# Two places of TensorE's program order in a long-convolution and soft-MoE kernel: transposes of the logits ahead of the inverse transform's first product, and the logits' products directly behind the dispatch products

## The chip, the core and the metric

The kernel runs on one NeuronCore of a Trainium2 chip. The core has TensorE (PE, matrix products; PEld is its weight load), VectorE (DVE), ScalarE (ACT), GpSimd (POOL), and SyncE (SP), whose queue issues nearly all DMA transfers here. The metric is the device time of one execution in microseconds (us). Three runs of the kernel before gave 859.84, 865.26 and 866.72 us; their median is 865.26 us.

## The reference

A batch of 8 sequences of 5696 tokens with 128 channels is convolved with a filter of the same length through Fourier transforms; the 45568 rows that result go through a soft mixture of experts with 32 slots. Everything is float32.

```python
Xf = np.fft.rfft(x, n=2 * S, axis=1); Hf = np.fft.rfft(h, n=2 * S, axis=0)
x = np.fft.irfft(Xf * Hf[None], n=2 * S, axis=1)[:, :S, :].reshape(B * S, D)
logits = x @ phi                          # (45568, 32)
d = np.exp(logits - logits.max(0)); d /= d.sum(0) + 1e-9
slot_input = d.T @ x                      # dispatch: sums over all tokens
for e in range(8): slot_out[e] = np.maximum(slot_input[e] @ w1[e], 0) @ w2[e]
c = np.exp(logits - logits.max(1)); c /= c.sum(1) + 1e-9
return c @ slot_out
```

## The kernel before

The transform of length N is split into 90 times 64 points and worked in three stages, each a set of matrix products on TensorE with a round through DRAM between them. The work is a software pipeline over steps t. The program order on every engine is the order in which the Python code issues instructions (a manual schedule), and each engine works its own list from the front.

**First stage** (`load_x`, `fold`, `first_low`, `first_high`; lines 195 to 226). Four columns of the input are loaded (L195), folded into sums and differences on GpSimd (L207), multiplied with a table (L217), copied out of PSUM by ScalarE into `fst` (L220) and stored to DRAM as `f` (L226).

**Second stage** (`stage_b1`, `stage_b2`). A unit loads `gt` from `f` (L249), makes products into the PSUM tile `bt` (L263), is multiplied with the filter's spectrum by four VectorE operations (two at L281, two at L290, ending in `yf`), is multiplied back on TensorE (L305), copied by ScalarE into `zst` (L311) and stored as `z` (L314). `slot_b` issues the first half of a new unit and then the second half of the unit before it, so the second half has to wait for `yf`. There are three units in two steps: one slot in an odd step, two in an even one. Each batch ends on a short unit of a quarter of the products.

**Third stage and soft MoE**, for a pair T of column groups, in two steps. In the odd step `stage_c1` waits for `zc` (L342, five DMAs of 1.15 MB in all into one single buffer), makes four products of two matrix products each (L361) in two parts, copies one half of each part with ScalarE (L370 into `y`, L374 into `om`) and combines the halves on VectorE (lines 366 and 367, once for `y`, once for `op` and `om`); GpSimd makes the rest of `y` (L380). In the even step `stage_c2` transposes `y` (L391, copies L393 into `yt`), `stage_c6` transposes the weights of the pair before the last (L504, copies L508), `dispatch` makes the slot sums of the pair before (L478, added by VectorE at L483), `stage_c3` makes the logits from `yt` and `phi` (L400, ScalarE copy into `lt` at L403), and `column_max` takes the running maximum over tokens on VectorE (L411, L416 into `low`, L419 into `df`). In the next odd step `stage_c4` transposes `lt` (L429), copies it into `L` (L433), takes the exponential `dt` with `low` as bias (L435) and that of `df` (L440), has GpSimd clear a corner of `dt` (L437), takes the maximum over slots on VectorE (L444) and subtracts it on GpSimd (L445). `stage_c5` transposes `dt` (L452, copy L455), and `softmax` finishes `L` (L460 to L466).

The order inside a step is given by strings of letters, one letter for one piece of the work, `ORDER_E` for odd steps and `ORDER_O` for even ones from step 9 on: `x` load of the input, `X` and `Y` first-stage products, `f` folds, `1`, `j` and `w` the first products, the second products and the combination of `stage_c1`, `4`, `b` (`slot_b`), `5`, `s` (softmax), `z` load of `zc`, `P` load of `gt`, `2`, `6`, `d` (dispatch), `3`, `m` (column maximum). Letters whose work does not exist in a step issue nothing. First-stage work ends before step 72; steps 72 to 79 still run second and third stage, and the step after them and the rest of the kernel (experts, output) are written out by hand.

All these products but L263's go to four rotating PSUM banks (`bank()`), so a bank is free once the reader of the tile four allocations earlier has finished.

Of the kernel before, what the change touches and what calls it, by code (L numbers as in the profile page):

```python
# [77 lines left out]
def kernel(  # L78
# [484 lines left out]
    for comp in range(2):  # L563
        fold(0, comp)
    wait_b2 = []
    ORDER_E, ORDER_O, FILL_E, FILL_O, XAHEAD = "xXYf14jwb5s", "zPxXfb26db3m", "xYfX14jwb5s", "zPxfXb26db3m", 3

    for t in range(last_front + 1):
        us = list(units(t))
# [286 lines left out]
```

## Time and profile before

| what | value |
|---|---|
| median of three runs | 865.26 us |
| the profiled execution's own time, and its span | 866.74 us, 864.4 us |
| busy in the span: PE, DVE, ACT, POOL | 89%, 72%, 51%, 43% |
| mean granted TensorE clock | 0.947 |
| moved by DMA | 271.99 MB, mean 315 GB/s |
| chain that ended last, by engine | PE 58%, DMA 21%, DVE 12%, SP's queue 3% |

A row of the timeline gives the start of a group of like instructions, its duration, engine, line, operation, tiles and count, and in brackets the idle time of the engine ahead of it with what ended that idle time. Matrix products overlap, so the time that a group takes on TensorE is read from its start to the start of the next group. A float32 product appears as two instructions, which is why eight are listed for four products.

### The profile page before, as it was taken

How to read it: one execution, taken by the hardware profiler on the slowest of the kernel's cores; microseconds unless marked ns; L12 is line 12 of the kernel's file. 1: busy time of each engine (PE TensorE's matmuls, PEld its weight loads, DVE VectorE, ACT ScalarE, POOL GpSimd, SP SyncE). 2: the span in 40 equal slices, each digit the busy share in tenths (PEclk: the TensorE clock that was granted, in tenths of full speed). 3: DMA queues.
4: the chain of work that ended last, by engine and by line, in shares of the span. 5: the costliest groups of instructions: out<-in, count | busy, mean ns of one | idle time of the engine just before them, and what ended most of it. 6: DMA issues, size and time to landing. Idle time of an engine off the chain costs nothing.

```text
span 864.4 us, 20502 instructions
## 1 busy us (share of the span) xinstructions
PE 769.7 (89%) x7796; PEld 374.4 (43%) x7796; DVE 626.5 (72%) x942; ACT 437.4 (51%) x967; POOL 374.8 (43%) x359
## 2 busy tenths in 40 slices
PE   5878888779999999999999999999978878978882
PEld 1222333234444444444444444444444444445882
DVE  3259867658777878887888788877778997973542
ACT  3422344435655655665566556656544545562531
POOL 2133424245556556665566555555533443540000
PEclk9999999989999999999999999999999999997755
DMA  9989999999999999999999999999997797760998
GB/s 294 294 268 308 306 319 342 337 335 331 329 323 343 343 349 318 343 337 340 325 336 345 320 339 330 348 312 335 334 333 264 265 316 277 283 276 8 371 380 327
DMA packets 153243, 271.99 MB, mean 315 GB/s; under 512 B 11878, under 2 KB 110054, under 8 KB 150005
## 3 DMA queue, kind: packets, MB, share of 16 engines
q1 hardware_dynamic: 152571, 270.38, 90.5%
q8 instruction: 62, 1.02, 0.4%
q10 hardware_dynamic: 576, 0.31, 0.1%
q14 instruction: 34, 0.28, 0.1%
HBM read 142.57 MB, written 127.98 MB: 313 GB/s over the span
## 4 chain that ended last, share of the span: by engine, by line
PE 58%; DMA 21%; DVE 12%; SPq 3%; issue 2%; ACT 1%; POOL 1%; DVEq 0%; ACTq 0%; POOLq 0%
PE bank L217 14%; PE bank L361 13%; PE bank L305 8%; PE bt L263 7%; PE bank L391 5%; DMA zc<-z 5%; DMA xc<-in_x_dram 5%; DMA out_dram<-o 5%; PE bank L478 3%; DMA gt<-f 3%; DMA xc<-in_h_dram 2%; DVE yf L290 2%; SPq L342 2%; DVE p L281 2%; DVE bt L281 2%
## 5 line engine op out<-in xcount | busy, mean ns | idle before, releaser
L207 POOL TENSOR_TENSOR x<-xc 128x512 f32<-128x512 f32 x126 | 158.0, 1276 | 245.0 <-PE bank L217 177.0
L217 PE MATMUL bank<-x,s 128*64 128x512 f32 (+1 forms) x1152 | 224.6, 610 | 14.0 <-DVE x L207 9.2
L311 ACT ACTIVATE zst<-bank 128x512 f32<-128x512 f32 (+1 forms) x184 | 98.6, 586 | 184.3 <-PE bank L305 165.1
L220 ACT ACTIVATE fst<-bank 128x512 f32<-128x512 f32 x216 | 127.4, 598 | 106.3 <-PE bank L217 87.6
L281 DVE TENSOR_TENSOR p<-bt,Hi 128x1024 f32<-128x1024 f32 x96 | 111.3, 1160 | 32.7 <-PE bt L263 31.6
L361 PE MATMUL bank<-zc,i 128*64 128x512 f32 x480 | 119.1, 618 | 12.4 <-DMA zc<-z 10.0
L305 PE MATMUL bank<-yf,vt 64*64 64x256 f32 x1440 | 100.8, 387 | 25.7 <-DVE yf L290 25.6
L263 PE MATMUL bt<-gt,wt 64*64 64x256 f32 x1620 | 114.3, 389 | 9.6 <-DMA gt<-f 8.1
L290 DVE TENSOR_TENSOR yf<-bt,p 128x512 f32<-128x512 f32 x192 | 119.4, 663 | 3.3
L217 PEld LDWEIGHTS bank<-x,s 128*64 128x64 f32 (+1 forms) x1152 | 55.8, 124 | 150.3 <-issue 79.9
L281 DVE TENSOR_TENSOR bt<-bt,Hr 128x1024 f32<-128x1024 f32 x96 | 113.0, 1177 | 0.0
L263 PEld LDWEIGHTS bt<-gt,wt 64*64 64x64 f32 x1620 | 54.2, 132 | 84.6 <-issue 33.1
L380 POOL TENSOR_TENSOR y<-y,op 128x512 f32<-128x512 f32 x64 | 77.6, 1212 | 13.4 <-DVE op L366 10.4
L305 PEld LDWEIGHTS bank<-yf,vt 64*64 64x64 f32 x1440 | 56.3, 134 | 57.4 <-issue 23.1
L366 DVE TENSOR_TENSOR y<-bank,y 128x512 f32<-128x512 f32 x32 | 22.1, 692 | 77.3 <-PE bank L361 73.8
L380 POOL TENSOR_TENSOR y<-y,om 128x512 f32<-128x512 f32 x54 | 64.1, 1187 | 2.1
L361 PEld LDWEIGHTS bank<-zc,i 128*64 128x64 f32 x480 | 30.9, 139 | 76.8 <-issue 46.6
L391 PE MATMUL bank<-ident,y 109*128 109x109 f32 x512 | 62.4, 272 | 1.3 <-DVE y L380 1.0
L391 PEld LDWEIGHTS bank<-ident,y 109*128 109x128 f32 x512 | 52.1, 147 | 17.2 <-issue 9.2
L393 ACT ACTIVATE yt<-bank 128x360 f32<-128x360 f32 x128 | 51.0, 490 | 2.4 <-PE bank L391 1.8
L809 PE MATMUL op<-so,cT 32*128 32x128 f32 x704 | 45.9, 379 | 5.7 <-ACT o L818 5.2
L466 POOL TENSOR_TENSOR L<-L,rs 128x512 f32<-128x512 f32 x32 | 33.6, 1051 | 31.1 <-DVE rs L465 20.9
(96 smaller groups left out, 792.0 us busy)
## 6 DMA issues: line engine op xcount, KB each, us to landing
gt<-f SPq DMA_DIRECT2D x99, 512.0 KB
z<-zst SPq DMA_DIRECT2D x88, 512.0 KB
f<-fst SPq DMA_DIRECT2D x144, 240.0 KB
zc<-z SPq DMA_DIRECT2D x30, 1024.0 KB
xc<-in_x_dram SPq DMA_DIRECT2D x64, 320.0 KB
f<-fst SPq DMA_DIRECT2D x144, 120.0 KB
out_dram<-o SPq DMA_DIRECT2D x16, 1024.0 KB
zc<-z SPq DMA_DIRECT2D x90, 128.0 KB
```

Of the source, the lines that this page charges most:

```text
L207: eng.tensor_tensor(out=folded(c, comp)[:, :, :], in0=t_[:, 0, :, :], in1=t_[:, 1, ::-1, :], op=AL.subtract if comp else AL.add)
L217: nc.tensor.matmul(p[o * width:(o + 1) * width, :], s1[:, comp + G, k], folded(c, comp)[:, :, :].rearrange("p n d -> p (n d)"), start=True ...
L220: nc.scalar.activation(st[:, :, G, :], p[:, :].rearrange("p (n d) -> p n d", d=D), AF.Copy)
L263: nc.tensor.matmul(bt[q * HP:(q + 1) * HP, a, o, :], wt[r, 2 * i + q, :], t_[r, 2 * o + q, :, :].rearrange("p c d -> p (c d)"), start=True ...
L281: nc.vector.tensor_tensor(out=p_, in0=pv, in1=h_, op=AL.mult)
L290: eng.tensor_tensor(out=y_[r, 0:k, c, :], in0=pv[:, :, c, :], in1=pi[r, 0:k, 1 - c, :], op=op_)
L305: nc.tensor.matmul(bz[q][a * HP:(a + 1) * HP, o * 2 * D:(o + 1) * 2 * D], vt[r, i, a, :], y_[r, a * m + o, :, :].rearrange("p c d -> p (c ...
L311: nc.scalar.activation(st[:, 0:m, q, :], bz[q][:, 0:m * 2 * D].rearrange("p (o x) -> p o x", o=m), AF.Copy)
L361: nc.tensor.matmul(p[h_ * HP:(h_ + 1) * HP, :], i1[0:kr, tab, :], t_[0:kr, h_, o, :, q, :], start=True, stop=True)
L380: eng.tensor_tensor(out=part_, in0=part(v, 0), in1=o_[:, :, :], op=sign)
L391: nc.tensor.transpose(p[:, i * TR:(i + 1) * TR], ys[T][0:TR, k * CH + i, 0:D], ident[0:TR, 0:TR])
L393: nc.scalar.activation(yt[:, k * CH:(k + 1) * CH, :, :], of_tokens(p), AF.Copy)
```

## The change

Two letters move, each by one place, in the strings for steps from 9 on; the strings for the steps before that are not touched.

```diff
-    ORDER_E, ORDER_O, FILL_E, FILL_O, XAHEAD = "xXYf14jwb5s", "zPxXfb26db3m", "xYfX14jwb5s", "zPxfXb26db3m", 3
+    ORDER_E, ORDER_O, FILL_E, FILL_O, XAHEAD = "xXYf41jwb5s", "zPxXfb26d3bm", "xYfX14jwb5s", "zPxfXb26db3m", 3
```

In odd steps `stage_c4` (L429 to L445) is issued ahead of the first part of `stage_c1` (L361, L370, L366, L367) and no longer between its two parts. On TensorE the eight L361 products become adjacent behind the four L429 transposes. On ScalarE the order L370, L433, L435, L440, L374 becomes L433, L435, L440, L370, L374. On VectorE L444 moves ahead of the first L366 and L367. In even steps `stage_c3` (L400, L403) is issued directly behind `dispatch` (L478) and ahead of the second `slot_b` (L263, L305, L281, L290, L311) and no longer behind it; on ScalarE L403 comes ahead of the two L311, and `column_max` stays behind the slot on VectorE. The lists of GpSimd and of SyncE with its DMAs are the same in both kernels. No instruction is added or removed.

## The prediction

> **What bounds the kernel now.** I read the page's slices first, then busy time by stretch, then the waits of TensorE and of SyncE's queue inside the stretch where all stages run, then the timelines there and in the steps after 72. The slices say that TensorE and the DMA engines are both nearly full from slice 9 to 28, about 190 to 630 us.
>
> ```profile
> PE   5878888779999999999999999999978878978882
> PEclk9999999989999999999999999999999999997755
> DMA  9989999999999999999999999999997797760998
> ```
>
> The busy time by stretch (columns: stretch, its length, then busy time and count of PE, PEld, DVE, ACT, POOL, then clock, DMA share, GB/s), one row for a batch of four pairs and two for a pair each in the steps from 72 on:
>
> ```profile
> 319.36:400.88 81.52, 80.31 (x825) 37.27 (x825) 64.93 (x100) 48.73 (x112) 47.75 (x45) 1.00 0.97 335
> 400.88:482.18 81.30, 80.30 (x824) 37.24 (x825) 65.01 (x100) 48.57 (x111) 47.33 (x45) 1.00 0.97 336
> ...
> 664.30:683.16 18.86, 16.20 (x184) 9.46 (x181) 16.88 (x26) 9.34 (x23) 6.87 (x7) 0.91 0.84 292
> 683.16:701.91 18.75, 16.09 (x185) 8.92 (x181) 16.87 (x26) 9.16 (x23) 6.85 (x7) 0.91 0.88 303
> ```
>
> In the full part a batch takes 81.3 to 81.5 us and TensorE idles about 1.0 us of it; the DMA share is 0.97. Who is ahead of whom is told by the waits of SyncE's queue from 238 to 606 us:
>
> ```profile
> SPq L195 <- DMA gt<-f: 34.5, 27, 2.0
> SPq L314 <- DMA gt<-f: 19.1, 17, 2.1
> SPq L195 <- DMA zc<-z: 16.8, 22, 2.5
> SPq L226 <- DMA z<-zst: 16.0, 23, 1.0
> ```
>
> These and the other rows that name a DMA add up to 117 of 368 us: the queue waits for earlier transfers to land. Rows that name an engine add up to 42 us, but most name one that cannot hold that transfer (a `z` store behind the `y` copy). Those that can (L226 behind its own `fst`, L314 behind `zst`, L195 behind the fold, L249 behind `bt`) are 1.8, 1.5, 2.8 and 0.9 us, 7.0 in all, 4% of the 159. The queue also runs behind the engines: the second slot's `zst` copies of one step were done at 438.1 us and their stores were issued from 441.9 on. So in the full part transfers run at their own pace and TensorE meets them at `zc`: it stood waiting ahead of L361 at 197.85, 218.21, 319.36, 400.88, 482.18, 523.12, 563.83 and 605.71 us for 0.28, 0.41, 0.68, 0.86, 0.66, 0.35, 0.58 and 1.24 us, 5.1 in all.
>
> From 72 on first-stage work is gone and VectorE sets the pace: TensorE idles 2.67 us in each pair until `yf`.
>
> ```profile
> 671.10 1.09 PE L263 MATMUL bt<-gt,wt 64*64 64x256 f32 x16
> 674.86 1.09 PE L305 MATMUL bank<-yf,vt 64*64 64x256 f32 x16 [2.67 <-DVE yf L290]
> ...
> 681.69 1.23 DVE L281 TENSOR_TENSOR p<-bt,Hi 128x1024 f32<-128x1024 f32 x1 [0.66 <-PE bt L263]
> ...
> 686.63 0.61 ACT L435 ACTIVATE dt<-lt,low 128x360 f32<-128x360 f32 x1 [0.31 <-DVE low L416]
> ```
>
> **The change, part by part.** Nothing is added or removed, so a gain can only be a change of geometry saved on TensorE or a wait covered, and a loss something queued behind a wait.
>
> *Products that become neighbours.* TensorE groups are priced from start to start. Four L361 products took 1.87 us ahead of the transposes (421.13 to 423.00) and 1.86 behind them (423.59 to 425.45), 3.73 in all. Late in the kernel, where eight follow one another, they took 3.58:
>
> ```profile
> 739.32 3.65 PE L361 MATMUL bank<-zc,i 128*64 128x512 f32 x16
> 742.90 1.72 PE L391 MATMUL bank<-ident,y 109*128 109x109 f32 x16
> ```
>
> That saves 0.15 us a pair. Dispatch takes 1.03 us ahead of L263 (434.01 to 435.04) and 0.91 in the one place where L400 follows it (718.45 to 719.36); L400 took 0.74 (436.93 to 437.67) and there 0.72. That saves 0.14. The first applies in 22 odd steps (29 to 71), the second in 21 even ones (30 to 70): 22 x 0.15 + 21 x 0.14 = 6.2 us of TensorE's time in the full part. The Trainium skill, "TensorE: Matmul & The Clock Gate", section "The mechanism" of Part 3, says that a weight load overlaps matrix products in flight only when it goes to another row group; by that both pairings, which use all 128 rows, would save nothing, and TensorE's 6.2 us would be 0. The rows above disagree with it.
>
> *Transposes L429 ahead of L361.* They need only `lt`, copied three microseconds earlier, and take 0.59 us (423.00 to 423.59). They move into the wait for `zc`; of the eight waits they can fill 0.28 + 0.41 + 0.59 + 0.59 + 0.59 + 0.35 + 0.58 + 0.59 = 4.0 us.
>
> Together the full part could give 10.2 us at one end. At the other it gives nothing: if the transfers keep their pace, `zc` lands when it did, and what TensorE saves becomes a longer wait ahead of L361. SyncE's list is unchanged and 96% of its waits are for its own transfers, so I am near that end: 4% of 10.2 is 0.4, and I take 0.5 us gained.
>
> *Step 73.* Here `zc` is late by 2.61 us (L361 at 644.75), and the clock is cold behind the wait: the transposes took 1.04 us (647.44 to 648.48). They go into the wait; with the saved change of geometry 1.2 us are gained, between nothing (if a later wait absorbs them) and 1.2. The next late thing is `yf` (656.06, waited for 2.28 us), which hangs on L361's end, so I take 1.2.
>
> *The pairs behind it, steps 74 to 79.* VectorE is busy without a gap from L281 of the second slot (662.83) through the maximum, the combinations and the next unit to `yf` at 674.7, and TensorE's slot waits for that. L400 now stands ahead of the L263 that starts this run: dispatch and L400 take 0.91 + 0.72 instead of dispatch's 1.03, so everything behind is 0.60 us later. Then L370: behind it in the old order stood the exponential L435, which waits for `low`; now L370 stands behind L435. In the row of 664 to 683, counted from L281's start at 662.83, `low` lets L435 start at +4.93, and L440 and then L374 followed at +5.44 and +5.53. L370 now takes that place, ends at +6.13, and VectorE's first L366 starts at +6.16 instead of +4.95. L444 runs inside that delay; the first L366 and L367 take 1.34 us (667.78 to 669.12), so the second L366 starts at +6.16 + 1.34 = +7.50 instead of +6.88 (669.71), 0.62 us later. So 1.22 us a pair, for three pairs (74/75, 76/77, 78/79): 3.7 us lost. The ends: 0 if L370's delay and L400 were covered, which no row suggests, and 2.6 a pair if the wait of 2.67 us, grown to 3.9, doubles the slow-clock stretch behind it (from 675.88 on L391 took 2.47 us where 431.82 to 433.55 shows 1.73, L504 0.87 for 0.46, L478 1.31 for 1.03: 1.4 us more); I take none of that, since the clock already drops at 2.67 us. The skill's same page, section "What's actually happening", puts the drop at an idle window of 3.4 us; by that the longer wait would be what crosses it, and the 1.4 us would come new in each pair, 4.2 us on the sum. The clock of 0.91 in these rows says it is paid already.
>
> *In the full part the same two delays must be checked.* L400 ahead of the slot makes `low` 0.60 us later: 441.0 becomes 441.6, while L435 can start, behind Y's last copy and L433, no earlier than 1.2 us after 441.3. That leaves 0.8 us. L370 then ends some 2.4 us after the transposes begin, when its partner product is just done, and the second L366 waits for its own product as before. The `zst` copies come 0.5 us later and their stores have 3.8 us to spare. PSUM banks: the second L361 product of the second part takes the bank of the transposes, freed by L433 two microseconds before; none is later than its product. I cost all this at nothing; if the 0.8 us were gone, it would be the drain's 0.62 us in every pair.
>
> **Sum**, against the profiled execution's 866.74 us: -0.5 - 1.2 + 3.7 = +2.0, or 868.7 us. That execution lies 1.5 us above the median of the runs shown; against the median the forecast is 867.2, rounded 867 us.
>
> **Rivals.** *The transfers follow TensorE.* If the 3% in which DMA engines rest can be used, a batch may fall from 81.4 towards 79.8 us, and over 5.3 batches up to 8.5 of the 10.2 us come through. For: the share reached 1.00 in single pairs, and a share below it means room. Against: the rows of SyncE's queue, full of waits for landings. With two thirds of it, 6 us: -6 - 1.2 + 3.7 = -3.5 from the median, 861.8, say 862 us. With all 8.5: 859 us. *Slower: L370 behind L435 in every pair.* One mechanism: the column maximum, late on VectorE, holds L435, and L370 and the first L366 queue behind it, so that `yf` is late at the first slot of the even step, where now there is nothing in hand (it stood waiting 0.35 us in one pair of four). It decides once `low` is over 0.8 us later than worked out, or L366's start over 0.4 us more. Price 0.62 x 22 = 13.6 us on top of the forecast: 881 us. For it: the drain shows L435 waiting for `low` by 0.3 us already. Against: VectorE stands idle 2.2 us ahead of the first L366 in the full part (423.19). *It does nothing anywhere*: the drain's delays are covered after all: 865.
>
> **How the numbers follow.** The forecast 0.51, the transfers' case 0.36, the slower case 0.08, nothing 0.05. The likeliest time is 867 us. The range goes from 860 (the transfers' case at most of its size) to 872 (the forecast with the slow-clock stretch, and the beginning of the slower case). A measurement of this kernel tells about 1% from no change. Over 1% faster (below 856.6) needs more than the whole of the transfers' case: 0.04. Over 1% slower (above 873.9) needs the slower case: 0.07. The rest, 0.89, is within 1%.
>
> **What would show it.** Right: batches still of 81.3 to 81.5 us with TensorE's wait ahead of L361 present in nearly every pair, its sum near 5 + 6 us; pairs from 664 us on of about 20.0 us with `yf` waits near 3.9; eight L361 products in 3.58 us; dispatch to L400 in 0.91. Wrong: batches of 80 us with few such waits (the transfers follow), `yf` waits in every even step of the full part (L370), or drain pairs still of 18.8 us.

## Result and profile after

The changed kernel took 867.84 us (median of 17 runs, 861.81 to 870.83), the kernel before, run beside it, 864.64 us (17 runs, 859.70 to 869.74). The ratio of the two is 1.0019 with a 95% interval of 0.9998 to 1.0040: between 0.2 us faster and 3.5 us slower, so no difference that this measurement can tell. The forecast was 867, a loss of 2 us. The profiled execution of the changed kernel took 869.63 us by its own time, with a span of 867.1 us.

Executions of one and the same kernel differ by up to 0.7% to either side. Ratios here and below are taken over all executions in the usual state and are not the quotients of the medians. The totals of single profiles are therefore not ranked below; what is compared is stretches inside them, and the ratios of many runs.

The slices of the page after the change:

```profile
PE   5888788789999999999999999999988778988882
PEclk9999999999999999999999999999999999989755
DMA  9889999999999999999999999999997887760999
```

As before, TensorE and the DMA engines are both nearly full between slices 9 and 28. One number of the page did move: VectorE is busy for 655.2 us instead of 626.5, with the same 942 instructions. That is the first sign of something that the prediction didn't have.

Busy time by stretch (columns as in the prediction: stretch, its length, then busy time and count of PE, PEld, DVE, ACT, POOL, clock, DMA share, GB/s), four batches of the full part and two pairs of the steps after 73:

```profile
237.82:320.12 82.30, 79.49 (x825) 38.03 (x825) 71.54 (x101) 50.40 (x115) 49.30 (x46) 1.00 0.97 332
320.12:400.78 80.66, 79.42 (x824) 38.02 (x825) 70.19 (x99) 48.05 (x109) 45.87 (x44) 1.00 0.97 335
400.78:482.58 81.80, 79.51 (x824) 38.41 (x825) 71.32 (x101) 50.31 (x115) 48.69 (x46) 1.00 0.97 337
482.58:566.60 84.02, 81.02 (x825) 38.70 (x825) 70.50 (x100) 48.07 (x109) 46.25 (x44) 0.98 0.96 326
...
664.27:684.34 20.07, 16.64 (x181) 9.43 (x180) 16.63 (x26) 9.14 (x23) 6.89 (x7) 0.91 0.89 316
684.34:704.41 20.07, 16.64 (x182) 9.64 (x181) 16.63 (x26) 9.25 (x23) 6.88 (x7) 0.91 0.83 283
```

In three of the four batches TensorE works 0.8 us less than the 80.3 of before (by the prediction's prices it would be 4 x 0.29 = 1.2), and the batch is still 81 to 84 us long at the same DMA share. VectorE works 70 to 71.5 us in a batch instead of 65. The pairs after 664 us take 20.07 us instead of 18.8.

For a table I cut both traces at the first L361 of step 29 (the second such group), of step 73 and of step 81. "Full part" is the first interval, "drain" the second, "tail" the rest.

| us | full part | drain | tail | idle ahead of L361 (full part, and step 73) | idle ahead of L305 (full part) |
|---|---|---|---|---|---|
| before | 446.90 | 76.43 | 143.24 | 7.66 in 9 places | 3.54 in 6 |
| after | 447.44 | 79.08 | 142.96 | 8.46 in 9 | 6.48 in 18 |

The start of the full part, 197.85 and 197.65 us, makes up the difference of the spans: -0.20 + 0.54 + 2.65 - 0.28 = +2.7 us. The loss is in the drain, and the full part took none of TensorE's saving. The waits of SyncE's queue from 238 to 606 us still begin with transfers that wait for transfers:

```profile
SPq L195 <- DMA gt<-f: 38.8, 29, 2.2
SPq L195 <- DMA zc<-z: 23.7, 30, 2.1
```

In the drain, the timelines of TensorE, VectorE and ScalarE show both delays that the prediction named:

```profile
675.58 1.73 PE L305 MATMUL bank<-yf,vt 64*64 64x256 f32 x16 [3.26 <-DVE yf L290]
...
681.15 0.79 PE L400 MATMUL bank<-yt,phi 128*32 128x360 f32 x8
681.87 1.09 PE L263 MATMUL bt<-gt,wt 64*64 64x256 f32 x16
...
669.10 0.69 DVE L366 TENSOR_TENSOR y<-bank,y 128x512 f32<-128x512 f32 x1 [0.50 <-ACT y L370]
...
667.89 0.61 ACT L435 ACTIVATE dt<-lt,low 128x360 f32<-128x360 f32 x1 [2.53 <-DVE low L416]
```

L400 starts 0.72 us ahead of L263. L435 waits for `low`, L370 stands behind it, and the first L366 waits for L370.

**What was new** stands in VectorE's row of the full part. Of all instructions of one line, durations in ns (least, median, most), first and last start and shape; first the changed kernel:

```profile
L416 DVE SCALAR_TENSOR_TENSOR low<-mx,low x31: 159/161/1194, 216.9 to 781.2; 128x1 f32<-128x1 f32 x31
```

and the kernel before:

```profile
L416 DVE SCALAR_TENSOR_TENSOR low<-mx,low x31: 159/159/160, 217.2 to 776.4; 128x1 f32<-128x1 f32 x31
```

A two-input operation on 128 single numbers takes up to 1.19 us where it took 0.16. This is so in 15 of the 22 pairs of the full part, and in the same 15 for L419 behind it: 15 x (1.03 + 1.04) = 31 us, which accounts for the 28.7 us by which VectorE's busy time grew (other lines took less, L464 by 1.3 us). One such place in the timelines of VectorE, GpSimd, ScalarE and TensorE after the change:

```profile
338.64 1.04 DVE L411 TENSOR_REDUCE mx<-lt 64x1 f32<-64x360 f32 x2
339.72 1.19 DVE L416 SCALAR_TENSOR_TENSOR low<-mx,low 128x1 f32<-128x1 f32 x1
340.94 1.20 DVE L419 TENSOR_TENSOR df<-low 128x1 f32<-128x1 f32 x1
...
342.90 0.69 DVE L366 TENSOR_TENSOR y<-bank,y 128x512 f32<-128x512 f32 x1 [0.16 <-ACT y L370]
...
339.62 2.50 POOL L207 TENSOR_TENSOR x<-xc 128x512 f32<-128x512 f32 x2 [5.97 <-PE bank L217]
...
341.01 0.61 ACT L435 ACTIVATE dt<-lt,low 128x360 f32<-128x360 f32 x1 [0.22 <-DVE low L416]
342.18 0.20 ACT L440 ACTIVATE dn<-df 128x1 f32<-128x1 f32 x1 [0.56 <-DVE df L419]
342.29 0.58 ACT L370 ACTIVATE y<-bank 128x512 f32<-128x512 f32 x1
```

GpSimd's two folds run from 339.62 to 342.12 us, 1.25 us each. L416 starts 0.1 us after the first and ends at 340.91, when that one is done; L419 starts beside the second and ends at 342.14 with it. All 30 long operations of this trace end 0.01 to 0.02 us behind the fold beside them. The same pair in the kernel before:

```profile
339.10 0.16 DVE L416 SCALAR_TENSOR_TENSOR low<-mx,low 128x1 f32<-128x1 f32 x1
339.30 0.16 DVE L419 TENSOR_TENSOR df<-low 128x1 f32<-128x1 f32 x1
...
339.75 2.51 POOL L207 TENSOR_TENSOR x<-xc 128x512 f32<-128x512 f32 x2 [6.10 <-PE bank L217]
```

There both were done at 339.46, 0.3 us ahead of the folds. Counted from the first dispatch product of the step, which is free of the shift between two executions, L416 starts 0.61 us later than before and the folds 0.14 us earlier, so L400 ahead of the slot moved it into the folds. Then L435 waits 0.22 us for `low`, L440 0.56 us for `df`, L370 ends late, and `yf` is 0.28 us late at the even step's first L305. The Trainium skill, "SBUF — State Buffer", section "Who interferes with whom", has this case: a VectorE instruction with two inputs in SBUF contends with a GpSimd instruction that reads SBUF, and the one that starts second stands until the first is done. The rows agree, to the 0.02 us above. They also agree with the other half of the rule, that an instruction with at most one SBUF input outside some modes is left alone: in the kernel before, L366, one of whose inputs is in PSUM, took its usual 0.69 us at 423.19 beside folds that ran from 421.26 to 423.76.

So three things were to be told apart: whether the transfers' pace, VectorE standing at the folds, or both kept the full part as long as it was; whether the drain's loss is the sum of the two delays; and whether the gain of step 73 is real.

### The profile page after: what moved, and what is told of

Its sections match the earlier page's. It is cut to its first block, busy times and chain, and to the rows that moved or that the text cites. A ratio compares the mean times of both kernels' runs of the same rounds, so it can differ in the third digit from the quotient of the medians.

```text
span 867.1 us, 20505 instructions
## 1 busy us (share of the span) xinstructions
PE 770.8 (89%) x7796; PEld 382.0 (44%) x7796; DVE 655.2 (76%) x942; ACT 440.0 (51%) x967; POOL 374.6 (43%) x359
## 2 busy tenths in 40 slices
DMA packets 153243, 271.99 MB, mean 314 GB/s; under 512 B 11878, under 2 KB 110054, under 8 KB 150005
## 4 chain that ended last, share of the span: by engine, by line
PE 44%; DVE 26%; DMA 18%; issue 4%; SPq 2%; ACT 2%; POOL 1%; DVEq 0%; POOLq 0%; ACTq 0%
PE bank L217 10%; PE bank L361 8%; PE bank L305 6%; PE bank L391 6%; DVE yf L290 5%; DVE p L281 5%; DMA out_dram<-o 5%; DVE bt L281 5%; PE bt L263 5%; DMA xc<-in_x_dram 4%; DMA zc<-z 3%; PE bank L478 3%; DMA f<-fst 2%; DVE om L367 2%; DVE op L366 2%
## 5 line engine op out<-in xcount | busy, mean ns | idle before, releaser
L217 PE MATMUL bank<-x,s 128*64 128x512 f32 (+1 forms) x1152 | 228.5, 618 | 15.0 <-DVE x L207 10.3
L311 ACT ACTIVATE zst<-bank 128x512 f32<-128x512 f32 (+1 forms) x184 | 98.6, 586 | 166.9 <-PE bank L305 152.2
L281 DVE TENSOR_TENSOR p<-bt,Hi 128x1024 f32<-128x1024 f32 x96 | 111.3, 1160 | 50.8 <-PE bt L263 50.1
L305 PE MATMUL bank<-yf,vt 64*64 64x256 f32 x1440 | 104.5, 387 | 30.6 <-DVE yf L290 29.8
L361 PE MATMUL bank<-zc,i 128*64 128x512 f32 x480 | 115.1, 622 | 11.2 <-DMA zc<-z 8.5
L290 DVE TENSOR_TENSOR yf<-bt,p 128x512 f32<-128x512 f32 x192 | 119.4, 663 | 3.3
L263 PE MATMUL bt<-gt,wt 64*64 64x256 f32 x1620 | 114.0, 389 | 6.6 <-DMA gt<-f 5.0
L281 DVE TENSOR_TENSOR bt<-bt,Hr 128x1024 f32<-128x1024 f32 x96 | 113.0, 1177 | 0.0
L263 PEld LDWEIGHTS bt<-gt,wt 64*64 64x64 f32 x1620 | 54.0, 132 | 92.0 <-issue 44.1
L305 PEld LDWEIGHTS bank<-yf,vt 64*64 64x64 f32 x1440 | 57.6, 134 | 63.9 <-issue 27.0
L361 PEld LDWEIGHTS bank<-zc,i 128*64 128x64 f32 x480 | 35.6, 141 | 69.7 <-issue 53.1
L391 PE MATMUL bank<-ident,y 109*128 109x109 f32 x512 | 64.9, 279 | 1.3 <-DVE y L380 1.0
L391 PEld LDWEIGHTS bank<-ident,y 109*128 109x128 f32 x512 | 54.7, 152 | 17.4 <-issue 11.4
L816 DVE COPY o<-op 128x512 f32<-128x512 f32 (+3 forms) x50 | 28.9, 627 | 25.2 <-DMA out_dram<-o 18.7
```

The costliest lines, as they stand in the source:

```text
L217: nc.tensor.matmul(p[o * width:(o + 1) * width, :], s1[:, comp + G, k], folded(c, comp)[:, :, :].rearrange("p n d -> p (n d)"), start=True ...
L263: nc.tensor.matmul(bt[q * HP:(q + 1) * HP, a, o, :], wt[r, 2 * i + q, :], t_[r, 2 * o + q, :, :].rearrange("p c d -> p (c d)"), start=True ...
L281: nc.vector.tensor_tensor(out=p_, in0=pv, in1=h_, op=AL.mult)
L290: eng.tensor_tensor(out=y_[r, 0:k, c, :], in0=pv[:, :, c, :], in1=pi[r, 0:k, 1 - c, :], op=op_)
L305: nc.tensor.matmul(bz[q][a * HP:(a + 1) * HP, o * 2 * D:(o + 1) * 2 * D], vt[r, i, a, :], y_[r, a * m + o, :, :].rearrange("p c d -> p (c ...
L311: nc.scalar.activation(st[:, 0:m, q, :], bz[q][:, 0:m * 2 * D].rearrange("p (o x) -> p o x", o=m), AF.Copy)
```

## Experiments

All ratios are against runs of the kernel before on the same chip. "Unhindered pair" is the time from one L361 group to the next where `zc` did not hold it and neither unit was a short one.

### The two halves of the change alone (e1, e2)

```diff
 # e1: only the transposes move
-    ORDER_E, ORDER_O = "xXYf14jwb5s", "zPxXfb26db3m"
+    ORDER_E, ORDER_O = "xXYf41jwb5s", "zPxXfb26db3m"
 # e2: only the logits' products move
+    ORDER_E, ORDER_O = "xXYf14jwb5s", "zPxXfb26d3bm"
```

> Only the odd step's part of the change: L429 to L445 ahead of the first part of stage_c1, L400 left behind the second slot. Theory V (VectorE and GpSimd get in each other's way: the running maximum L416, L419 now falls into GpSimd's folds L207 and takes 1.19 us each instead of 0.16, so the first L366 and yf are late and this eats what TensorE saves): the maximum is not later here, L416 and L419 stay at 0.16 us, no yf wait of 0.28 us a pair; 22 pairs x 0.15 = 3.3 us less in the full part, 1.2 less at step 73, 3 x 0.62 = 1.9 more in steps 74 to 79: 2.6 us faster than before, ratio 0.997. Theory T (transfers keep their pace, what TensorE saves becomes a wait ahead of L361): full part 0, so 0.7 us slower, ratio 1.001.

> Only the even step's part: L400, L403 ahead of the second slot, L429 left between the two parts of stage_c1. V: the maximum is 0.6 us later, so L416 and L419 are long again (1.19 us) in three pairs of four; but L370 does not stand behind them, and VectorE has 2.2 us of idle time ahead of L366, so at most 0.3 us a pair is late: full part between -2.9 and 0, steps 74 to 79 3 x 0.60 = 1.8 slower: ratio 0.999 to 1.002. T: full part 0, 1.8 us slower, ratio 1.002. Both: pairs from 664 us on about 19.4 us long.

Measured: e1 866.93 us, ratio 1.0009 (0.9978 to 1.0041); e2 868.24 us, ratio 1.0043 (1.0009 to 1.0077). L416 and L419 are long in no pair of e1 and in 15 of e2: the move of L400 alone brings them into the folds. The unhindered pair is 20.10 us in e1 and 20.12 in e2 against 20.26 before, 0.16 and 0.14 us, which are the 0.15 and 0.14 priced for the two new neighbourhoods. In e1 the full part took 446.95 us with 10.06 us of waits ahead of L361, in e2 443.58 with 5.69. e1's ratio is that of the transfers' theory (1.001) and lies above the other's 0.997. In e2, although the maximum is long, TensorE waits for `yf` 6 times for 3.54 us in the full part, as before: the long L416 and L419 cost something only together with the other half of the change, which puts L370 behind L435 and L440.

In the drain the two delays separate cleanly. From L281 of one unit to the L305 of the next, the stretch in which VectorE sets the pace, it is 12.03 us before and in e2, 12.61 in e1 and after: L370 behind L435 is 0.58 us. From that L305 to the next L263, TensorE's own stretch, e2 and after show 0.61 us more than before and e1 where the clock is alike: that is L400. What follows: the prediction's two sizes (0.62 and 0.60) hold, each with the half that it was put down to. The two ratios don't rank the halves, since their intervals overlap, and e2's profile, at 861.3 us of span, was of one of its shortest executions.

### The change until step 72, the old order behind it (e3)

```diff
+    LATE_E, LATE_O = "xXYf14jwb5s", "zPxXfb26db3m"
-        for c_ in ((ORDER_E if full else FILL_E) if t % 2 else (ORDER_O if full else FILL_O)):
+        for c_ in ((LATE_E if t >= NA else ORDER_E if full else FILL_E) if t % 2
+                   else (LATE_O if t >= NA else ORDER_O if full else FILL_O)):
```

> The whole change, but from step 72 on the old order of both strings. Both theories: what the change costs behind step 73 (2.65 us from L361 at step 73 to L361 at the end of the steps) is gone, and so is the 1.2 us gained at step 73 itself; pairs from 664 us on again 18.8 us, yf waits 2.67 us. The full part is as with the change. About 1.5 us faster than the change, ratio to before 1.000. If the ratio stays at 1.002, the loss sits in the full part and not in the steps from 72 on.

Measured: 868.32 us, ratio 1.0024 (0.9989 to 1.0058). The drain took 73.81 us, 5.3 less than after and 2.6 less than before, the last part because the granted clock fell three times in this drain and five times in that of before (a pair of 18.23 us here, where the pair of before at 664 us, of 18.86, has 1.4 us of cold clock behind the wait for `yf`). The full part was 448.56 us, with 11.52 us of waits ahead of L361. So undoing the change behind step 72 takes the drain's delays away, and the full part does not give anything even then. The expectation had said that a ratio that stays at 1.002 would put the loss into the full part. The ratio did stay, but its interval holds the expected 1.000 as well, and the full part's 448.56 us against 446.90 is within the scatter of single executions, so this run does not decide that.

### The maximum ahead of the slot as well (e4)

```diff
-    ORDER_O = "zPxXfb26d3bm"
+    ORDER_O = "zPxXfb26d3mb"
```

> The change with column_max (L411 to L419) moved ahead of the second slot too (d, 3, m, b), so that the maximum is done some 3 us earlier and cannot meet GpSimd's folds, nor hold L435. V: L416, L419 0.16 us everywhere, no yf wait in the full pairs, which fall from 20.34 towards 19.97 us; full part 6 us faster than before and part of the 4 us of zc waits covered; steps 74 to 79 about 0.4 us a pair slower than before; step 73 1.2 faster: 6 to 10 us faster, ratio 0.989 to 0.993. T: full pairs get waits ahead of L361 instead, batches stay at 81.4 us: ratio 0.999 to 1.000.

Measured: 869.04 us, ratio 1.0033 (1.0001 to 1.0066), slower than either theory had it. The profile is of the longest of its 12 executions (873.21 us), so its totals count for less than its rows; e10 below repeats the full part. L416 and L419 take 0.16 us everywhere, TensorE's waits for `yf` are back at 3.50 us in 6 places, and the unhindered pair is down to 19.97 us, 0.29 below before. Yet the full part took 448.04 us, and the waits ahead of L361 rose to 14.72 us in 12 places. What follows: the long L416 is not what kept the changed kernel from gaining. With it gone, TensorE waits for `zc` by as much as it has saved. In the drain the maximum stands ahead of the spectrum products on VectorE, which sets the pace there, and it took 80.79 us (in e8 below 78.45 us, where the order before takes 71.51; part of that difference is the clock, which fell four times in e8's drain and never in the other): there the old order is the better one.

### Half of the input's bytes (e6, e7, e8)

If the transfers set the full part's pace, fewer bytes must let TensorE's saving through, and show the folds' price beside it. Three orders were run that load only half of the bytes of each column of the input from column 3 x NJ on (8.75 of 272 MB less; the order of the transfers stays).

```diff
+            ns = 2 if c < 3 * NJ else 1
-                        ap=[v.ap[0], [gap * D, 2], [1, CH * D]])
+                        ap=[v.ap[0], [gap * D, ns], [1, CH * D]])
```

> The kernel before, but from the third sequence of input columns on load_x brings in only the first of the two halves of each tile (xc[:, 0]); the second half keeps what an earlier load left. That leaves out half of the input's bytes, about 0.36 of 6.6 MB a pair, and changes no order, no engine instruction and no number of DMAs. Theory T (transfers keep their pace): TensorE's waits for zc ahead of L361, 7.7 us in the profile of before, mostly go; pairs stay at 20.26 us, where TensorE sets the pace: 5 to 8 us faster than before, ratio 0.991 to 0.994. If the waits stay, they are not due to how much is moved.

> The change, with half of the input's bytes left out in the same way. T: the waits ahead of L361 (8.5 us) mostly go, and what is left is VectorE: L416 and L419 still meet GpSimd's folds (1.19 us each in three pairs of four), the pairs stay at 20.34 us with yf waits of 0.28 us, no better than before's 20.26; with 2.6 us lost from step 73 on: 3 to 6 us faster than before with full input, ratio 0.993 to 0.997, and no faster than before with half the input.

> The change with column_max ahead of the second slot, and half of the input's bytes left out in the same way. T: its waits ahead of L361 (14.7 us with full input) mostly go and TensorE's saving comes through: pairs 19.97 us instead of 20.26, full part 433 to 436 us instead of 439: 9 to 13 us faster than before with full input, ratio 0.985 to 0.990, and 4 to 6 us faster than before with half the input. If it is no faster than before with half the input, TensorE's saving is lost to something else than transfers.

| | median us, ratio to before | full part us | waits ahead of L361 | unhindered pair us | L416 long |
|---|---|---|---|---|---|
| order before (e6) | 851.83, 0.9852 (0.9814 to 0.9889) | 439.17 | 1.42 | 20.26 | 0 of 21 |
| order after (e7) | 856.46, 0.9887 (0.9852 to 0.9923) | 438.71 | 0.44 | 20.34 | 15 of 21 |
| with the maximum ahead of the slot (e8) | 851.03, 0.9824 (0.9789 to 0.9859) | 432.84 | 0 | 19.97 | 0 of 22 |

TensorE's waits from 190 to 630 us (lines are one higher here; total, times, longest) in the order before:

```profile
PE bank L306 <- DVE yf L291: 3.5, 6, 1.8
PE bank L362 <- DMA zc<-z: 1.2, 1, 1.2
```

in the order after:

```profile
PE bank L306 <- DVE yf L291: 7.8, 21, 1.8
```

and with the maximum ahead of the slot:

```profile
PE bank L306 <- DVE yf L291: 3.5, 6, 1.8
```

The waits for `zc` are all but gone in all three, and now the orders differ. With the maximum out of the folds' way the whole saving arrives: 439.17 - 432.84 = 6.3 us, against the 6.2 that the prediction counted from instructions. With the order of the change nothing arrives (0.5 us): the saving of 6.2 us is eaten by `yf`, late in 15 pairs by 20.34 - 19.97 = 0.37 us, 5.6 us in all. So the full part of the changed kernel has two limits, and each of them alone takes the saving: the transfers, and VectorE behind the folds.

The whole times were not what was expected. All three kernels were faster than forecast (0.991 to 0.994, 0.993 to 0.997 and 0.985 to 0.990): in e6 the full part began 4.1 us earlier and the drain was 4.9 us shorter than before, which the expectation had left out. And e8 was to be 4 to 6 us faster than e6, but the two medians differ by 0.8 us: e8's drain, 6.9 us longer, takes what its full part gained.

### The folds out of the way, the maximum as late as in the change (e9)

One thing was open: whether the folds do this, or simply the maximum's being 0.6 us late.

```diff
 # half of the input's bytes as above, and
-    ORDER_E, ORDER_O = "xXYf41jwb5s", "zPxXfb26d3bm"
+    ORDER_E, ORDER_O = "xXY4f1jwb5s", "zPxXfb26d3bm"
```

> The changed kernel's order, but in odd steps the folds stand behind the transposes of the logits and what belongs to them (GpSimd starts L207 later), and half of the input's bytes are left out in the steps before 72 as in the two half-input kernels before, so that transfers hold nobody and the columns computed from the missing half are not the reference's. The maximum over columns stays behind the slot, exactly as late as in the changed kernel. Theory (L416 and L419 stand because a fold of GpSimd is running when they come, and the late L370 and yf follow from that): both take 0.16 us in nearly all pairs instead of 1.19 and 1.20, TensorE's waits for yf ahead of L305 in the full part fall from 7.8 us in 21 pairs towards 3.5 in 6, a pair takes 19.97 us instead of 20.3, and the stretch from the first L361 of step 29 to that of step 73 takes about 433 us instead of the 438.7 of the changed order with half the input; the time is some 5 us under that kernel's, a ratio of 0.982 to 0.984 to the kernel before. Rival (the maximum is simply 0.6 us later and L435, L370 and the first L366 queue behind it whatever GpSimd does): L416 and L419 may be short, but yf is still late by about 0.3 us in some 20 pairs, the stretch takes 438 to 439 us and the ratio stays near 0.989.

Measured: 852.39 us, ratio 0.9845 (0.9805 to 0.9886); the full part took 434.00 us, the unhindered pair 19.97. TensorE's waits from 190 to 626 us (beside one of 0.4 us ahead of L361), and the maximum and the fold in the timelines of VectorE and GpSimd:

```profile
PE bank L306 <- DVE yf L291: 3.5, 6, 1.8
```

```profile
332.20 0.16 DVE L417 SCALAR_TENSOR_TENSOR low<-mx,low 128x1 f32<-128x1 f32 x1
332.39 0.16 DVE L420 TENSOR_TENSOR df<-low 128x1 f32<-128x1 f32 x1
...
335.23 2.51 POOL L208 TENSOR_TENSOR x<-xc 128x512 f32<-128x512 f32 x2
```

The maximum is where the change puts it, the folds begin 3 us behind it, and both short operations take 0.16 us. All but 1.2 us of what e8 gained in the full part is there. It is the folds: being late costs nothing as long as no fold is running. The ratio lies 0.0005 above the expected 0.982 to 0.984, well within its interval; the full part's 434.00 is 1 us above the expected 433.

### A version made of the findings (e10)

Transposes first and maximum ahead of the slot until step 71, the transposes first in step 73 too, the old order in step 72 and from 74 on, all of the input:

```diff
+    ORDER_E, ORDER_O = "xXYf41jwb5s", "zPxXfb26d3mb"
+    LATE_E, LATE_O = "xXYf14jwb5s", "zPxXfb26db3m"
+        late = t == NA or t > NA + 1
+        for c_ in ((LATE_E if late else ORDER_E if full else FILL_E) if t % 2 else
+                   (LATE_O if late else ORDER_O if full else FILL_O)):
```

> All of the input. Until step 71 and in step 73 the transposes of the logits stand ahead of the first product as in the changed kernel, and the logits' products AND the maximum over columns stand ahead of the slot (which kept L416 and L419 at 0.16 us); in step 72 and from step 74 on both strings are the old ones. Theory (in the full part the transfers keep their pace whatever TensorE saves; behind step 72 VectorE sets the pace and the old order is the shorter one there): the stretch from the first L361 of step 29 to that of step 73 takes 447 to 448 us as in every kernel with all of the input, with TensorE's waits ahead of L361 near 15 us instead of 7.7; step 73 gains about 1.2 us, the pairs behind it take 18.9 us (18.2 with a warm clock) as before and not 20.07; ratio 0.9985 to 1.000, hardly to be told from no change. Rival (the transfers follow TensorE once no fold is in the way of the maximum): the stretch falls by 4 to 6 us and the ratio is 0.992 to 0.995.

Measured: 866.08 us against 865.76 us (17 runs), ratio 0.9978 (0.9945 to 1.0012): not told from no change. The interval just reaches the slow end of the rival's 0.992 to 0.995; what speaks against the rival is the full part, which was to fall by 4 to 6 us. It took 446.91 us, that of before to 0.01, with 13.17 us of waits ahead of L361 in 14 places; the pairs behind step 73 took 18.22, 17.88 and 18.25 us (warm clock). Busy time over a stretch of this kernel, columns as above, with all of the input:

```profile
240.00:400.00 160.00, 156.05 (x1636) 75.80 (x1636) 130.13 (x200) 95.67 (x220) 94.20 (x88) 1.00 0.97 333
```

and of the order with the maximum ahead of the slot, with half of the input's bytes:

```profile
240.00:400.00 160.00, 159.29 (x1664) 76.34 (x1660) 131.32 (x202) 97.51 (x223) 96.06 (x90) 1.00 0.94 325
```

The same instructions in the same order: TensorE works 156.05 of 160 us at a DMA share of 0.97, and 159.29 at 0.94. That is the transfers' limit in two rows.

Step 73 did not give its 1.2 us here. It took 20.93 us where before took 19.55: TensorE, early, waited 3.70 us for `zc` instead of 2.61, and in the seven us from 646.00 the granted clock was 0.60 (before: 0.76). It stood at half from 644.78 to 651.60 us, and in the kernel before only from 645.73 to 649.14. The timeline of TensorE shows eight L361 in 6.33 us instead of 3.65:

```profile
646.16 6.33 PE L361 MATMUL bank<-zc,i 128*64 128x512 f32 x16 [3.70 <-DMA zc<-z]
```

The drain was still 1.2 us shorter than before, by the warm clock of the pairs behind, and that comes and goes from execution to execution of several kernels.

## Why the prediction held, and where it did not

The sum was +2.0 us, to 867.2; the median was 867.84, 3.2 us above that of the runs beside it, the ratio says +1.6 us (-0.2 to +3.5), the two profiles +2.7. Step by step:

- **The products that become neighbours.** Predicted: eight L361 in 3.58 us, dispatch to L400 in 0.91, 6.2 us of TensorE's time in the full part. Measured: 3.58 and 0.91, and 6.3 us where nothing else was in the way (the order before against e8, half the input). Right. The sentence of the Trainium skill's section "The mechanism" by which the same pairings would have saved nothing is not what these runs show. (The section also lets a load into "the background weight buffer" go ahead; which of the two happened here no run shows.)
- **The transfers keep their pace, 0.5 of 10.2 us gained.** Right, and shown as far as single executions of each kernel go: e10 spares TensorE 0.29 us in every pair and has nothing else in the way, and its full part is that of before, with longer waits for `zc`. With 3% fewer bytes the saving comes through. A full part that is 0.5 us longer instead of 0.5 shorter is within what single executions differ by. (The rows of SyncE's queue that name an engine add up to 44.5 us and not to 42; the share stays 4%.)
- **L361's waits near 5 + 6 us.** Wrong in the changed kernel. Until step 71 they were 6.5 us (8.46 less step 73's 1.99), not 11. The rest of TensorE's saving stood at L305, in 18 waits for `yf` of 6.48 us instead of 6 of 3.54. In e10, without the folds' trouble, they are 9.5 (13.17 less step 73's 3.70).
- **"I cost all this at nothing."** This is the step that failed. The prediction counted 0.60 us of delay for `low` and found a margin of 0.8 us left behind it, and e9, where the maximum is short, has just these 0.80 us between `low` and L435. But it took the durations of L416 and L419 from the trace of before as fixed. Moved by 0.6 us they fell into the folds and took 1.19 and 1.20 us: `low` was ready 1.65 us later in the pair shown, 0.25 more than 0.60 and the margin together, and `df`, which the prediction did not follow, held L440 and L370 for longer still. With it came the sign that the prediction had named for the slower rival, waits for `yf` in even steps (15 pairs of 22), by 0.37 us a pair and not 0.62. The sum did not show it, because in the full part the transfers had already taken what it costs: 5.6 us out of a saving that could not be used. That the forecast of the time stands in spite of this step is luck.
- **Step 73, 1.2 us gained.** In the changed kernel the pair took 19.18 us instead of 19.55 with the 0.61 us of L400 inside it, so about 1.0 was gained, by the stretch from L361 to L263 (5.28 instead of 5.91) and smaller ones. In e1 and e10, which have the same transposes ahead, the pair took 21.06 and 20.93 with waits of 3.47 and 3.70 us for `zc`. There the clock stood at half for 6.8 us (644.82 to 651.65 in e1) and in the changed kernel for 3.4 (645.18 to 648.59). How late `zc` is does not decide it: e3, with the old order in this step, waited 4.05 us, had 3.4 us at half clock and took 18.26 us. The price was one execution's.
- **The drain, 1.22 us a pair and 3.7 in all.** Right: 0.61 for L400 in three pairs and 0.58 for L370 in three make 3.6, and less about 1.0 in step 73 they make the 2.65 measured from step 73 to 81. The pairs took the 20.07 us forecast as about 20.0. The `yf` wait grew to 3.26 us and not to 3.9, because L400 stands ahead of both VectorE's run and TensorE's way to L305 and so moves both ends of the wait; only L370's part lengthens it.
- **No more cold clock in the drain.** Right for these two executions: 1.4 us of it in the pair at 664 us, as before, at the same granted clock of 0.91. But the length of the wait, by which the prediction argued, does not decide it alone: in e1 one pair with a wait of 2.54 us took 19.45 us and the next, with the same 2.54, 18.02. What else decides is shown below.
- **The rivals.** "The transfers follow TensorE" fell with e10's full part, not with its ratio. The slower case happened as a mechanism and not as a price. "It does nothing anywhere" fell with the drain's rows.

**When the clock falls.** In each of the eleven traces the granted clock changes only at points that lie a multiple of 3.41 us apart, and it falls to half when TensorE has idled long enough between two of them. Three such intervals of e1 (columns as above):

```profile
675.54:678.95 3.41, 1.46 (x21) 1.03 (x21) 3.31 (x7) 0.34 (x1) 2.70 (x4) 1.00 0.95 301
678.95:682.37 3.42, 3.42 (x26) 3.13 (x28) 2.99 (x4) 2.71 (x9) 0.68 (x1) 0.50 0.98 381
692.61:696.02 3.41, 1.79 (x24) 0.93 (x20) 3.38 (x4) 2.09 (x4) 3.33 (x3) 1.00 0.37 134
```

The first wait of 2.54 us left 1.95 us of idle time in one interval, and the next interval ran at 0.50. The second wait was split by a point into 1.62 and 0.93 us, and the clock stayed at 1.00. Of the intervals at full clock from 190 to 718 us in the eleven traces, all 38 with 1.82 us or more of idle time were followed by half clock, and none with 1.74 us or less; in between, both happened. Where the points lie differs from execution to execution. The rule that the prediction weighed (the Trainium skill, "TensorE: Matmul & The Clock Gate", section "What's actually happening": the clock drops after an idle window of about 3.4 us, and the windows run freely) agrees with the 3.41 us; but half an idle window was enough here.

What stays open: why e2's full part took 443.58 us, the shortest of all with the whole input. It may be the scatter of one execution; 12 runs of e2 give no gain. But e2 spares TensorE about 2.9 us there, and 3.3 us less is what it would take if in that execution the transfers had followed.

## What to carry to other kernels

When a kernel has two resources close to full, a saving on one is worth only what the other leaves: price it at the pace of the slower, and test it by taking a few per cent of load off the other. When an instruction is moved, look at what runs on the neighbouring engines at its new time, because the duration in the old trace holds for its old neighbours: a VectorE operation with two inputs in SBUF, however tiny, can take as long as the GpSimd operation beside it. A move that helps where TensorE is the bound should end where another engine takes over.

## What the runs showed of the hardware

- VectorE's operations on 128 x 1 numbers took 1.19 and 1.20 us instead of 0.16 when a GpSimd fold of 1.25 us had begun ahead of them, and ended 0.01 to 0.02 us behind the fold (30 operations of the changed kernel). With the folds 3 us behind (e9) they took 0.16.
- The granted clock changed only at points a multiple of 3.41 us apart, and fell to 0.50 behind every interval in which TensorE had idled 1.82 us or more (38 of 38 from 190 to 718 us) and none with 1.74 or less. So a wait of 1.86 us inside one interval halved it (e3, from 695.50 us), and one of 2.66 us, split into 1.15 and 1.52 by a point, did not (e3, at 676.53).
- With the clock at half for two such intervals (644.78 to 651.60 us in e10), eight L361 products took 6.33 us instead of 3.65.
- Transfers of 3.2% fewer bytes (8.75 of 272 MB) and 2.4% fewer packets (3738 of 153243) shortened the full part of the kernel before by 7.7 us, of which 7.2 were waits ahead of L361, and moved the DMA share only from 0.97 to 0.93.
